# Infini-attention with a gated one-token FFN on one core: sums in a bank each, five jobs per unit, masks two blocks at a time, another clock for the planner, another prologue and output order

## The chip, the cores and the metric

The kernel runs on one core of a Trainium2 chip. The metric is device time in microseconds (us) of one launch; smaller is better. A profile is one execution, with the time of every instruction on each engine: TensorE (PE for matmuls, PEld for its weight loads), VectorE (DVE), ScalarE (ACT), GpSimd (POOL) and SyncE (SP), which here issues all transfers.

## The reference

Two branches over the same 2048 tokens of width 640, mixed by a gate for each token:

```python
x = A_x                                              # [1, 2048, 640]
g = sigmoid((x * gate_w).sum(-1, keepdims=True))
# A: 32 heads of 20 columns, 4 segments of 512 tokens, a memory M, z carried over segments
for s in range(4):
    qs, ks, vs = q[:, :, s], k[:, :, s], v[:, :, s]  # x @ wq, x @ wk, x @ wv
    logits = einsum("bhqd,bhkd->bhqk", qs, ks) * scale + mask
    a_dot = einsum("bhqk,bhkd->bhqd", softmax(logits), vs)
    a_mem = (phi(qs) @ M) / (phi(qs) @ z + 1e-6)
    outs.append(gh * a_mem + (1 - gh) * a_dot)       # gh = sigmoid(beta), by head
    M = M + phi(ks).T @ vs; z = z + phi(ks).sum(tokens)
a = concat(outs) @ wo
# B: the one token with the largest x @ w_r goes through a SwiGLU FFN (640 -> 1728 -> 640)
b = x + scatter(y * sigmoid(r_sel))
out = g * a + (1 - g) * b
```

The mask is additive: -1e9 for `ar[:, None] < ar[None, :]`, that is, for every key that lies behind its query.

## The kernel before

Every matrix is split into a high and a low part (`hi` rounded by ACT, `lo` the difference by DVE or POOL), and a product is the sum of three matmuls: high by high, low by high, high by low.

**Units and jobs.** A unit is half of the heads in one segment: eight units. Its projections (`projections`, `pair_up`) come in four jobs. Jobs 0 and 1 make two tiles each of 128 channels (queries and keys of four heads mixed, `TILES`) by 512 tokens; jobs 2 and 3 each make a half of the fifth channel tile, as two pieces of 128 tokens, and then two blocks of 128 tokens of the values (320 columns, 322 in the first half, where the router and the gate ride along). `pair_up` works on the two halves of the PE array's rows at once: a pair is one matmul on rows 0 to 63 and one on rows 64 to 127, each into a bank of its own; after 15 pairs (5 row blocks by 3 products) the halves change banks, with a drain of PE between them ("swap"), and 15 more pairs follow. Both banks belong to one tile, `sums`.

**Evacuation.** When a job is done, `evac_t` copies the channel tiles to SBUF (ACT for the first bank, L417, DVE for the second, L420), and `evac_v` the values (ACT L518, DVE L522). The next job's first matmul waits for that. High and low parts then go through HBM (`place`, `place_low`, `bring_back`) into `qs` and `ks`, where a group of four heads has its stacked operands; there are five such pairs of buffers.

**Attention.** For each group n (32 in all) five steps `a_step` make the logits in one orientation (L622), add the mask on the diagonal block with four matmuls of 128 columns (L626: `pick` loaded as weights, `tri` streamed), and DVE takes the row maximum (L629). The maxima go through a transpose and four small transfers (`m_rows`, `qs<-mr`) into two more rows of `qs`. Five steps `b_step` then make the transposed logits with the maximum subtracted (L677), ACT exponentiates (L681), POOL masks (L687), and `pv_step` multiplies by the values (L702). Of the five steps of a group, two have one block of 512 columns, two have blocks of 384 and 128, one has two of 256.

**Planner.** The order on every engine is fixed when the program is built: a loop at the end keeps a rough clock for PE, ACT, DVE, POOL and a single transfer stream (`now`), and at each point takes a logit step, a matmul pair of the current job, a pv step, a chore (memory read `nm` and write `mp`, normalisation `otp`, key transposes `ktp`) or a step of the FFN, `Side`. A transfer is issued as soon as its source is due by that clock; SP's own time is not counted. The engines then wait for one another by semaphores.

**Output.** When the FFN has ended, `out_stage` multiplies 16 tiles of 128 tokens by `wo`: rows are fetched back, transposed (`ttp`, L918), split, and multiplied in a `pair_up` of 320 columns a bank; DVE mixes both banks into the output row (L981), one after the other. The transposes of the next tile stand in the swap of the current one.

**Prologue.** The constants (`identf`, `pick`, `tri`, `gate`, `mask4`, memsets) come first on DVE and POOL; the first loads use a ring of four buffers, `raw`.

## Time and profile before

| | us |
|---|---|
| median of 3 runs (787.68 to 788.91) | 787.73 |
| the profiled execution | 790.6 |
| its span, first to last instruction | 788.9 |
| PE busy in the span | 698.2 |
| DVE, ACT, POOL busy | 406.1, 366.0, 267.4 |
| mean granted clock of TensorE | 0.932 |

PE is busy in 88% of the span. A busy time counts from the start of a matmul to the end of its pipeline, so two matmuls overlap; what a matmul costs in a stream is the distance from its start to the next one's start. The granted clock is 1.0 at 2.4 GHz and 0.5 at 1.2 GHz.

### The profile page before, as it was taken

The page shows a single profiled execution, that of the slowest core. Times are in us where ns is not written, and L with a number is a line of the kernel's source. Part 1 is how long each engine was busy: PE and PEld are TensorE (multiplying, and loading weights), DVE is VectorE, ACT ScalarE, POOL GpSimd, SP SyncE. Part 2 cuts the span into 40 slices and gives each one's busy share as a digit, 9 for nine tenths or more (in the row PEclk, how much of TensorE's full clock was granted, in tenths as well). Part 3 has the DMA queues.
Part 4 walks back from the last instruction along what each step waited for, and adds up shares of the span by engine and source line. Part 5 has one row for each costly group of instructions (what it writes and reads, how often), then busy time and mean ns, then how long its engine had stood idle before and what let it go on. Part 6 is the DMA issues. An engine that isn't in the chain of part 4 may idle for free.

```text
span 788.9 us, 19342 instructions
## 1 busy us (share of the span) xinstructions
PE 698.2 (88%) x7860; PEld 576.9 (73%) x7860; DVE 406.1 (51%) x730; ACT 366.0 (46%) x646; POOL 267.4 (34%) x343
## 2 busy tenths in 40 slices
PE   2889999999999999989999898987998959898886
PEld 1678778777877787778778786777777847777675
DVE  7435554554546346464665344662656545553433
ACT  3624545554546356654655354451554425334411
POOL 5514322543244455832533143251445212111100
PEclk9969998999999889999999899995999978999999
DMA  4783545245424554778476536553348644243451
GB/s 118 209 256 111 140 124 145 87 129 145 137 61 105 159 151 129 205 211 223 134 229 208 162 98 199 156 143 108 120 140 229 187 149 124 87 129 123 136 160 51
DMA packets 84912, 116.69 MB, mean 148 GB/s; under 512 B 36624, under 2 KB 48408, under 8 KB 84824
## 3 DMA queue, kind: packets, MB, share of 16 engines
q1 hardware_dynamic: 84824, 115.46, 51.1%
q8 instruction: 62, 1.02, 0.5%
q14 instruction: 26, 0.21, 0.1%
HBM read 72.94 MB, written 41.96 MB: 146 GB/s over the span
## 4 chain that ended last, share of the span: by engine, by line
PE 75%; DMA 9%; DVE 7%; issue 3%; ACT 3%; SPq 1%; POOL 0%; DVEq 0%; ACTq 0%; POOLq 0%
PE sums L359 41%; PE pv L702 8%; PE a L622 5%; PE a L626 5%; PE bt L677 5%; DMA qs<-mr 3%; PE nm L475 3%; PE otp L729 3%; DVE mx L629 2%; PE mp L498 2%; PE ttp L918 1%; DVE xf L981 1%; DMA stkq<-lo 1%; ACT p L681 1%; DMA ks<-stkk 1%
## 5 line engine op out<-in xcount | busy, mean ns | idle before, releaser
L629 DVE TENSOR_REDUCE mx<-a 128x2 f32<-128x1024 f32 (+3 forms) x256 | 202.0, 821 | 177.0 <-PE a L626 175.1
L681 ACT ACTIVATE p<-bt 128x1024 f32<-128x1024 f32 x160 | 164.2, 1027 | 147.2 <-PE bt L677 142.1
L687 POOL TENSOR_SCALAR_AFFINE_SELECT p<-p 128x512 f32<-128x512 f32 (+1 forms) x160 | 88.2, 552 | 294.4 <-ACT p L681 285.7
L359 PE MATMUL sums<-xhi,whi 64*128 64x128 f32 (+1 forms) x640 | 131.8, 371 | 20.9 <-ACT xhi L164 12.2
L359 PE MATMUL sums<-xhi,wlo 64*128 64x128 f32 (+1 forms) x640 | 129.1, 359 | 3.1 <-DVE wlo L167 3.1
L359 PE MATMUL sums<-xlo,whi 64*128 64x128 f32 (+1 forms) x640 | 129.7, 361 | 0.0
L622 PE MATMUL a<-ks,qs 60*128 60x384 f32 (+3 forms) x512 | 100.4, 361 | 22.8 <-DVE mx L629 13.3
L359 PEld LDWEIGHTS sums<-xhi,whi 64*128 64x128 f32 x640 | 79.0, 205 | 34.4 <-issue 13.0
L626 PEld LDWEIGHTS a<-tri,pick 64*128 64x128 f32 x1024 | 100.7, 201 | 3.6
L626 PE MATMUL a<-tri,pick 64*128 64x128 f32 x1024 | 97.4, 264 | 0.0
L677 PE MATMUL bt<-qs,ks 62*128 62x384 f32 (+3 forms) x512 | 81.3, 341 | 15.4 <-DMA qs<-mr 12.8
L622 PEld LDWEIGHTS a<-ks,qs 60*128 60x128 f32 x512 | 59.5, 199 | 37.3 <-issue 21.3
L359 PEld LDWEIGHTS sums<-xhi,wlo 64*128 64x128 f32 x640 | 81.0, 207 | 6.4 <-POOL xlo L167 3.6
L359 PEld LDWEIGHTS sums<-xlo,whi 64*128 64x128 f32 x640 | 81.2, 207 | 5.8 <-POOL xlo L167 0.6
L702 PE MATMUL pv<-p,va 128*32 128x512 f32 (+3 forms) x1024 | 75.5, 435 | 0.4 <-ACT mr L658 0.4
L677 PEld LDWEIGHTS bt<-qs,ks 62*128 62x128 f32 x512 | 53.8, 196 | 24.5 <-DMA qs<-mr 11.7
L429 POOL TENSOR_TENSOR lo<-phi,hi 128x512 fp32r<-128x512 f32 (+1 forms) x48 | 53.1, 1107 | 46.7 <-ACT hi L425 30.4
L359 PE MATMUL sums<-whi,xhi 64*128 64x322 f32 (+1 forms) x320 | 64.1, 366 | 1.6
L359 PE MATMUL sums<-whi,oh 64*128 64x320 f32 x320 | 55.1, 330 | 10.5 <-DVE xf L981 8.3
L702 PEld LDWEIGHTS pv<-p,va 128*32 128x32 f32 x1024 | 30.2, 109 | 43.4 <-issue 35.3
L359 PE MATMUL sums<-wlo,xhi 64*128 64x322 f32 (+1 forms) x320 | 60.8, 342 | 0.0
L359 PE MATMUL sums<-whi,xlo 64*128 64x322 f32 (+1 forms) x320 | 60.7, 340 | 0.0
(110 smaller groups left out, 1096.0 us busy)
## 6 DMA issues: line engine op xcount, KB each, us to landing
qs<-stkq SPq DMA_DIRECT2D x64, 240.0 KB
ks<-stkk SPq DMA_DIRECT2D x64, 240.0 KB
raw<-in_xT_dram SPq DMA_DIRECT2D x40, 256.0 KB
stkq<-hi SPq DMA_DIRECT2D x24, 320.0 KB
otok<-ou SPq DMA_DIRECT2D x32, 160.0 KB
xf<-in_x_dram SPq DMA_DIRECT2D x8, 640.0 KB
out_dram<-xf SPq DMA_DIRECT2D x16, 320.0 KB
wt<-in_wg_dram SPq DMA_DIRECT2D x10, 432.0 KB
```

The costliest lines, as they stand in the source:

```text
L359: nc.tensor.matmul(o, a, b, start=phase == 0 and i == 0, stop=phase == 1 and i == n - 1)
L429: nc.gpsimd.tensor_tensor(out=lo, in0=c, in1=f32(hi), op=OP.subtract)
L475: nc.tensor.matmul(nm[:, c, :], e[:GC, 128 * c:128 * c + 128], mbd[:, g, :], start=True, stop=True)
L498: nc.tensor.matmul(mp[:, g, :], kk[:, g, c, :], va[u % 2][:, c, GW * g:GW * g + GW], start=c == 0, stop=c == 3)
L622: nc.tensor.matmul(a[:, b, at:at + w], q_, ks[n % NS][64 * b:64 * b + ST, p, :w], start=True, stop=False)
L626: nc.tensor.matmul(a[:, b, at + w - 128:at + w], pick[r, h], tri[r, h], start=False, stop=h == 1)
L629: nc.vector.tensor_reduce(out=mx[n][:, :, p, i:i + 1], in_=a[:, :, at:at + w], axis=AX.X, op=OP.max)
L677: nc.tensor.matmul(bt[:, b, at:at + w], k_, qs[n % NS][64 * b:64 * b + ST + 2, p, L - w:], start=True, stop=True)
L681: nc.scalar.activation(pt, bt, AF.Exp, scale=SCALE)
L687: nc.gpsimd.affine_select(out=d, in_=d, pattern=[[0, e[1]] for e in dims[:-1]] + [[1, 128]], base=0, channel_multiplier=-1, compare_op=OP. ...
L702: nc.tensor.matmul(pv[32 * j:32 * j + 32, 128 * c:], va[u % 2][:, c, VW * h:VW * h + 32], pt_tiles[n, j % 2, c][:, j // 2], start=c == 0, ...
L729: nc.tensor.transpose(tp[:, c].rearrange("p j r -> p (j r)"), o[:, 128 * c:128 * c + 128], identf)
```

## The change

- **Two tiles.** `sums` becomes two tiles, `sums` and `sumt`, of one bank each. ACT evacuates the first and DVE the second, for channels and for values alike.
- **Five jobs.** The fifth channel tile has a job of its own, two pieces of 256 tokens; jobs 3 and 4 make the values.
- **Masks.** A step with two blocks adds both masks at once: four matmuls that stream 2 x 128 columns, instead of eight of 128. The step with two blocks of 256 reduces them in one DVE instruction.
- **Clock.** `now` gets SP, and `dma` counts 0.45 us of SP for an issue and bytes by 260 GB/s for the transfer; what follows is due by that. Transfers wait until SP is free by the clock and go by rank, the maxima's first. In the last 1.2 us of a job no logit step is taken. Chores and the FFN's steps have conditions and due times of their own; the FFN no longer has to end before the output stage starts.
- **Prologue.** The first nine loads are issued and split before the constants; the first six use the ring of `p`.
- **Output.** High-part products come first, then the ten with the low part; DVE mixes the first bank while ACT scales the second, and POOL adds that one; transposes for the next tile come before a tile's matmuls or in its swap.

```diff
+PR = 6
+FIRST = 18
+JOBS = 5
...
+    def dma(dst, src, kb):
+
+        nc.sync.dma_start(dst, src)
+        now["SP"] = max(now["SP"], now["PE"]) + 0.45
+        now["DMA"] = max(now["DMA"], now["SP"]) + kb / 260
+        return now["DMA"] + 2.2
...
     def flush_dmas(t):
-        for e in sorted((e for e in dmas if e[0] <= t), key=lambda e: e[0]):
+        while now["SP"] <= t + 0.2:
+            e = min((e for e in dmas if e[1] <= t), key=lambda e: e[:2], default=None)
+            if e is None:
+                break
             dmas.remove(e)
-            e[1]()
+            e[2]()
...
-    sums = psum.tile([128, 2, 512], F32, name="sums")
+    sums = [psum.tile([128, 512], F32, name=n) for n in ("sums", "sumt")]
...
-        dst = c.rearrange("p (a b) -> p a b", a=2) if len(src.shape) == 3 else c
-        if scalar:
-            nc.scalar.copy(dst, src)
-            free = run("ACT", 0.17 + w / 1200, now["PE"])
-        else:
-            nc.vector.tensor_copy(dst, src)
-            free = run("DVE", 0.12 + w / 960, now["PE"])
+        for bank, t0, t1 in parts:
+            if bank == 0:
+                nc.scalar.copy(c[:, t0:t1], sums[0][:, :t1 - t0])
+                end = run("ACT", 0.17 + (t1 - t0) / 1200, now["PE"] + 0.22)
+            else:
+                nc.vector.tensor_copy(c[:, t0:t1], sums[1][:, :t1 - t0])
+                end = run("DVE", 0.15 + (t1 - t0) / 960, now["PE"] + 0.22)
...
+        copy, engine = ((nc.scalar.copy, "ACT"), (nc.vector.tensor_copy, "DVE"))[bank]
+        copy(sub(va[u % 2], c * (HH * VW + 11), [[VW * q, 2], [VW, q], [1, DH]]),
+             sub(acc, 0, [[VC // 2 + (2 if hf == 0 else 0), 2], [DH, q], [1, DH]]))
...
-            for job in range(4):
+            for job in range(JOBS):
...
+                if job < 2:
+                    n, f, g = L, channels(u, 2 * job, 0, L), channels(u, 2 * job + 1, 0, L)
+                elif job == 2:
+                    n, f, g = L // 2, channels(u, 4, 0, L // 2), channels(u, 4, L // 2, L // 2)
+                else:
+                    n, f, g = w, tokens(u, c, w), tokens(u, c + 1, w)
...
+        ends = [at + w - 128 for i, p, at, w in LOGITS[k]]
+        for h in range(2):
+            for b in range(2):
+                r = slice(64 * b, 64 * b + 64)
+                if k < 2:
+                    nc.tensor.matmul(a[:, b, ends[0]:], pick[r, h], tri[r, h], start=False, stop=h == 1)
+                else:
+                    nc.tensor.matmul(sub(a[:, b], min(ends), [[max(ends) - min(ends), 2], [1, 128]]), pick[r, h],
+                                     sub(tri[r, h], 0, [[0, 2], [1, 128]]), start=False, stop=h == 1)
...
-        later_dma(now["ACT"], fn)
+        later_dma(now["ACT"], fn, 0)
...
-                    k, part = divmod(i, 3)
+                    k, part = divmod(i, 2) if i < 2 * KT else (i - 2 * KT, 2)
...
+            nc.vector.scalar_tensor_tensor(out=x0, in0=sums[0][:, :n], scalar=R["gx"][:, t:t + 1], in1=x0,
+                                           op0=OP.mult, op1=OP.add)
...
+            nc.scalar.activation(half, sums[1][:, :n], AF.Copy, scale=R["gx"][:, t:t + 1])
...
+            nc.gpsimd.tensor_tensor(out=x1, in0=half, in1=x1, op=OP.add)
...
     def both():
         yield from projections()
-        for f in side:
-            while f.live:
-                f.step()
         yield from out_stage()
...
+    for _ in range(9):
+        load_next()
+    for _ in range(9):
+        split_next()
+    constants()
+    now["PE"] = at["T", 0, 0]
...
-        if logits(0.0, t):
+        if (where[0] != "mid" or left[0] > 1.2) and logits(0.0, t):
             continue
```

Three places of the order. On PE, the end of unit 1's second job and the start of its third, before (`a` and `bt` are the two logit orientations, `tri` by `pick` the masks):

```order
L359 MATMUL sums<-xlo,whi 128x512 x2
L677 MATMUL bt<-qs_114,ks_115 128x512 x2
L622 MATMUL a<-ks_118,qs_117 128x256 x2
L626 MATMUL a<-tri,pick 128x128 x4
L622 MATMUL a<-ks_118,qs_117 128x256 x2
L626 MATMUL a<-tri,pick 128x128 x4
L677 MATMUL bt<-qs_114,ks_115 128x384 x2
L677 MATMUL bt<-qs_114,ks_115 128x128 x2
L359 MATMUL sums<-xhi,whi 128x128 x2
```

The same place on PE after:

```order
L371 MATMUL sums<-xlo,whi 128x512
L371 MATMUL sumt<-xlo,whi 128x512
L653 MATMUL a<-ks_94,qs_89 128x384 x2
L653 MATMUL a<-ks_94,qs_89 128x128 x2
L662 MATMUL a<-tri,pick 128x2x128 x4
L717 MATMUL bt<-qs_88,ks_93 128x512 x2
L371 MATMUL sums<-xhi,whi 128x256
L371 MATMUL sumt<-xhi,whi 128x256
```

Eight mask matmuls have become four wider ones, the pair behind them has 256 columns instead of 128, and one logit step fewer stands between the two jobs.

On DVE, the last of the constants and the first splits in the prologue, before (`ogate`, `ed`, `mask`, `ks` are constants, `wlo` and `xlo` low parts of the first loads, `phi<-sums` evacuates the first job):

```order
L106 TENSOR_SCALAR ogate<-gate 128x32
L112 TENSOR_SCALAR ed<-jd 80x80
L114 TENSOR_REDUCE mask_106<-ed 80x4
L121 MEMSET ks_109 128x1024
L121 MEMSET ks_115 128x1024
L121 MEMSET ks_121 128x1024
L167 TENSOR_TENSOR wlo<-raw,whi 128x5x48
L167 TENSOR_TENSOR wlo<-raw,whi 128x5x16
L167 TENSOR_TENSOR xlo<-raw,xhi 128x512 x3
```

The start of DVE's queue after:

```order
L175 TENSOR_TENSOR wlo<-raw,whi 128x5x80
L175 TENSOR_TENSOR wlo<-raw,whi 128x5x32
L175 TENSOR_TENSOR wlo<-raw,whi 128x5x80
L175 TENSOR_TENSOR wlo<-raw,whi 128x5x64
L175 TENSOR_TENSOR xlo<-raw,xhi 128x512 x3
L108 TENSOR_SCALAR identf<-jp 128x128
L110 MEMSET ks_92 128x1024
L110 MEMSET ks_94 128x1024
```

The splits have moved ahead of the constants, and the constants now stand ahead of the first job's evacuation on DVE.

On PE, the swap of the last output tile that still has transposes in it, before (`ttp` are the transposes of the next tile's rows):

```order
L359 MATMUL sums<-whi,ol 128x320 x2
L918 MATMUL ttp<-identf,ot 128x128 x4
L918 MATMUL ttp<-identf,ot_10943 128x128
L359 MATMUL sums<-whi,oh 128x320 x2
L359 MATMUL sums<-wlo,oh 128x320 x2
```

The last transposes on PE after:

```order
L371 MATMUL sums<-whi,ol 128x320
L371 MATMUL sumt<-whi,ol 128x320
L964 MATMUL ttp<-identf,ot 128x128 x4
L964 MATMUL ttp<-identf,ot_9891 128x128
L371 MATMUL sums<-whi,oh 128x320
L371 MATMUL sumt<-whi,oh 128x320
```

They have moved from the middle of a tile to the gap between two tiles, and the low parts (`ol`) are the last products of a half.

## Rows read from the trace of the kernel before

**Rows 1.** The page's first part: busy us, share of the span, instructions.

```profile
PE 698.2 (88%) x7860; PEld 576.9 (73%) x7860; DVE 406.1 (51%) x730; ACT 366.0 (46%) x646; POOL 267.4 (34%) x343
```

**Rows 2.** PE's timeline: start us, length us, line, output<-inputs, shape, count, [idle before].

```profile
37.86 0.27 PE L359 MATMUL sums<-xhi,wlo 64*128 64x128 f32 x2
...
39.20 0.28 PE L359 MATMUL sums<-xhi,wlo 64*128 64x128 f32 x2
39.31 0.27 PE L359 MATMUL sums<-xlo,whi 64*128 64x128 f32 x2
39.67 0.33 PE L359 MATMUL sums<-xhi,whi 64*128 64x128 f32 x2
```

**Rows 3.** PE's timeline, a transposed logit step and the projection pair behind it.

```profile
77.05 0.41 PE L677 MATMUL bt<-qs,ks 62*128 62x384 f32 x4
77.29 0.46 PE L359 MATMUL sums<-xlo,whi 64*128 64x512 f32 x2
```

**Rows 4.** PE's timeline, two logit steps with two masks each.

```profile
61.22 0.34 PE L622 MATMUL a<-ks,qs 60*128 60x256 f32 x2
61.40 0.34 PE L626 MATMUL a<-tri,pick 64*128 64x128 f32 x4
...
61.92 0.28 PE L359 MATMUL sums<-xlo,whi 64*128 64x128 f32 x2
...
75.44 0.29 PE L622 MATMUL a<-ks,qs 60*128 60x256 f32 x2
...
76.07 0.46 PE L359 MATMUL sums<-xhi,wlo 64*128 64x512 f32 x2
```

**Rows 5.** PE's timeline around the first job's end.

```profile
26.72 0.41 PE L359 MATMUL sums<-xlo,whi 64*128 64x512 f32 x2
28.53 0.50 PE L359 MATMUL sums<-xhi,whi 64*128 64x512 f32 x2 [1.40 <-DVE phi L420]
```

**Rows 6.** Groups by shape: count | busy us, mean ns of one | idle us before.

```profile
L417 ACT COPY phi<-sums 128x512 f32<-128x512 f32 x16 | 9.3, 584 | 14.9 <-PE sums L359 14.9
L420 DVE COPY phi<-sums 128x512 f32<-128x512 f32 x16 | 11.0, 690 | 16.3 <-ACT phi L417 15.9
```

**Rows 7.** PE's waits: engine, line <- what released it: us, times, longest.

```profile
PE a L622 <- DVE mx L629: 13.3, 9, 7.3
PE bt L677 <- DMA qs<-mr: 12.8, 5, 4.7
PE sums L359 <- DVE xf L981: 8.3, 11, 1.2
PE a L622 <- DVE rg L522: 7.5, 7, 1.5
PE sums L359 <- DVE phi L420: 4.9, 7, 1.4
```

**Rows 8.** Windows at half clock: us, busy (x) PE PEld DVE ACT POOL, PEclk.

```profile
115.62:122.43 6.81, 6.81 (x66) 6.72 (x64) 1.51 (x5) 2.80 (x6) 2.80 (x4) 0.50 0.29 78
...
sum 105.59, PE 92.57 PEld 86.07 DVE 36.44 ACT 32.12 POOL 28.79; mean PE 7.71 PEld 7.17 DVE 3.04 ACT 2.68 POOL 2.40
```

**Rows 9.** The chain that ended last: start us, us, what, count; output tiles.

```profile
769.20 2.48 PE sums L359 x30
...
772.86 2.47 PE sums L359 x30
...
779.79 2.47 PE sums L359 x30
```

**Rows 10.** Timelines of ACT and DVE in the prologue.

```profile
5.11 3.43 ACT L164 CAST whi<-raw 128x400 fp32r<-128x400 f32 x6 [0.75 <-DMA raw<-in_wc_dram]
10.45 0.62 ACT L164 CAST xhi<-raw 128x512 fp32r<-128x512 f32 x1 [1.90 <-DMA raw<-in_xT_dram]
...
1.18 4.48 DVE L89 TENSOR_SCALAR identf<-jp 128x128 f32<-128x128 int32 x1 [1.18 <-POOL jp L87]
...
13.62 0.91 DVE L121 MEMSET ks<- 128x1024 f32 x1 [0.16 <-issue]
```

More of the change, by code (lines that the diff above doesn't have):

```diff
@@ L139, in run @@
+    now = {"PE": 0.0, "ACT": 0.0, "DVE": 0.0, "POOL": 0.0, "SP": 0.0, "DMA": 0.0}
     def run(engine, us, *ready):
@@ L165, in split @@
         end = run("ACT", 0.2 + width / 1200, ready)
-        fast = now["DVE"] + 1.0 < now["POOL"] and key[1] == 0 and key[0] != "O"
+        fast = now["DVE"] + width / 960 < now["POOL"] + width / 430 and issued[0] <= FIRST
         (nc.vector if fast else nc.gpsimd).tensor_tensor(out=lo, in0=raw, in1=f32(hi), op=OP.subtract)
@@ L266, in feed @@
     def feed():
[L268 removed]
+        while room() and max(raw_free[raw_slot()], now["SP"] - 0.2) <= now["PE"]:
             load_next()
@@ L365, in place @@
-    def place(kind, m, c0, hi, r0, n, t0, t1, ready):
+        left[0] = 2 * n * us_of(cols)
+        for phase in range(2):
+            if phase:
+                where[0] = "swap"
+                yield 0.0
+                nc.tensor.drain()
+                pe(0.12)
+            use((64, 128))
+            where[0] = "mid"
+            for i in range(n):
+                for o, f, r in ((o0, f0, phase), (o1, f1, 1 - phase)):
+                    a, b, ready = f(i, r)
+                    pe(0.0, ready)
+                    nc.tensor.matmul(o, a, b, start=phase == 0 and i == 0, stop=phase == 1 and i == n - 1)
+                note(phase, i)
+                left[0] -= us_of(cols)
+                yield pe(us_of(cols)) - 0.22
@@ L902, in out_mix @@
         nc.scalar.activation(xf[t], xf[t], AF.Copy, scale=R["gb"][:, t:t + 1])
-        end = run("ACT", 0.85, now["DMA"])
+        end = run("ACT", 0.85, xf_at[t])
         nc.vector.scalar_tensor_tensor(out=xf[t], in0=R["yb"], scalar=R["oh"][:, t:t + 1], in1=xf[t], op0=OP.mult,
@@ L936, in fetch_rows, with ahead @@
             row_load(t)
-            ot_at[t] = now["PE"] + 3.0
+            return True
+    def ahead(t):
+        fetch_rows(t)
+        fetch_rows(t + 1)
+        if t in ot and ot_at[t] <= now["PE"] and misc_ready(2) <= now["PE"] + 0.4:
+            out_rows(t)
             return True
@@ L1101, in tile_infini_mod @@
         blocked = next_b() is None and done_b[0] < NG
-        old = [e for e in chores if e[0] <= t]
-        if pv and (where[0] == "open" or blocked or gt > 1e8 or left[0] > 2.0):
+        old = [e for e in chores if e[0] <= t and e[-1]()]
+        if pv and (where[0] == "open" or blocked or gt > 1e8 or left[0] > 2.0 or over[0] == JOBS * NU):
             logits(0.2, t)
@@ L1106, in tile_infini_mod @@
             continue
-        if old and where[0] == "swap":
+        waits = t - side_at[0] if side and side[0].last == 2 else -1.0
+        if where[0] == "swap" and (old or waits >= 0.0) and misc_ready() <= t + 0.2:
             logits(0.2, t)
@@ L1116, in tile_infini_mod @@
             continue
-        if logits(0.4 if gt < 1e8 else 99.0, t):
+        if logits(1.0 if gt < 1e8 else 99.0, t):
             continue
-        if old and gt > 1e8:
+        if gt > 1e8 and (old or waits >= 0.0) and misc_ready() <= t:
             visit(9.0, False)
```

408 lines of the change are left out of this document (200 added, 208 removed).

## The prediction

> **What bounds the kernel now.** I read the page's first part, then PE's waits, then PE's timeline. PE is busy for 698.2 of the span's 788.9 us, DVE for 406.1, ACT for 366.0 [rows 1]: PE sets the end, and a microsecond taken from it counts almost in full. Three things make its time long. First, its matmuls: a stream of 128-column pairs moves on by (39.20 - 37.86) / 12 = 0.112 us a pair [rows 2], while the two pairs of a transposed logit step, 512 columns in all, take 77.29 - 77.05 = 0.24 [rows 3], so 0.12 a pair of 256. A 128-column pair costs nearly as much as one of twice the width. Second, waits: 90.7 us in which PE has nothing in it, the largest behind DVE's maxima, the maxima's transfers and the evacuations [rows 7]. Third, the clock: in twelve stretches, together 105.6 us with 92.6 us of PE busy, it is granted at half, 1.2 GHz [rows 8]; at 2.4 GHz that work takes half, so the clock costs 46.3 us.
>
> I sum against the span, 788.9 (device time of that execution 790.6), and take the saving from the median of the runs, 787.73.
>
> **A. The fifth channel tile: -25.** Before: 8 units x 2 jobs x 2 halves x 15 = 480 pairs of 128 columns, 480 x 0.112 = 53.8. After: 240 pairs of 256. No projection pair of 256 is in the trace; the nearest row is the logit pair at 0.12 [rows 3], 28.8 us; the dearest is the pair of 256 ahead of a mask, 61.40 - 61.22 = 0.18 [rows 4], 43.2. So -25.0, between -11 and -25. I take the first: like it, the new pairs follow their own kind. A rule of the Trainium skill weighs against this term: "TensorE: Matmul & The Clock Gate", section "Back-to-back issue gap", gives the isolated spacing as 134 cycles for 128 columns and 262 for 256, with the caution that it leaves out the weight loads; by it two narrow matmuls cost what one wide one does, and A would be under 1 us in an estimate from that page. The trace sides with the caution: 0.112, not half of it.
>
> **B. The masks: -15.** Of 160 steps 96 have two blocks. One costs 0.70 (61.22 to 61.92) or, behind a wide pair, 0.63 (75.44 to 76.07) [rows 4]; mean 0.66. After: the same four logit matmuls, 0.24 as in [rows 3], and two mask pairs of 256 columns at 0.12 to 0.18: 0.48 to 0.60. I take 0.50, since nothing hinders the weights of the second pair: 96 x 0.16 = -15, between -6 and -17. That the moving operand repeats its 128 columns by a stride of zero is not in the trace; if it cost a pair more, the upper end holds.
>
> **C. Drains and changes of shape: +2.** A swap costs 39.67 - 39.31 = 0.36 against 0.11, so 0.25 [rows 2]; one fewer per unit, -2.0. By the order PE changes its tile shape (64 x 128, 128 x 128, 128 x 32) 206 times instead of 165; each at something between nothing and that 0.25, taken at 0.1: +4, at most +10.
>
> **D. Job starts: -6.** Now 1.81 us lie between a job's last pair and the next job's first [rows 5], most of it ACT's copy (584 ns) and then DVE's (690 ns), one after the other [rows 6]. Side by side it is 1.81 - 0.58 = 1.23, of which the pair itself is 0.23. The order puts one or two logit steps there (a step of two masks 0.50, a transposed one 0.24), some 0.7 us, so 0.3 stay open at 40 starts: 12 us, against 4.9 + 7.5 + (13.3 - 7.3) = 18.4 in three rows now [rows 7]. That the last 1.2 us of a job take no logit step keeps an exponential or a maximum from standing ahead of the evacuation. Bounds: -14 if no start waits, +8 if as much again opens.
>
> **E. Output tiles: -11.** A tile of the undisturbed end takes 779.79 - 772.86 = 6.93: two halves of 2.47, a swap, and 772.86 - 771.68 = 1.18 of evacuation [rows 9]. DVE's two equal instructions become one beside ACT, about -0.5, and the transposes fill what is left of that gap instead of widening the swap by some 0.7: -1.1 on each of the last five tiles. On the other eleven, where logit steps fill the gaps, half of that. POOL's addition lies behind the banks' release and hides, but for the last tile's, under 1 us. Bounds -4 and -17 (all sixteen).
>
> **F. Transfers that PE waits for: -13.** 12.8 us are waits of the transposed logits for the maxima's transfers, and 7.3 us one wait of a logit step on DVE [rows 7], whose queue was held by the FFN's last transfer. Both are orders in which the rough clock did not see SP's queue; now it counts SP, sends the maxima first, and issues DVE's addition only when its transfer is due. I take two thirds of 20.1; bounds -5 and -20. What it counts, 0.45 us an issue, may be short.
>
> **G. Prologue: -3.** Now the first activation is cast at 10.45, 1.9 us late, though the weights' casts end at 5.11 + 3.43 = 8.54 [rows 10]; with nine loads under way at once it would follow at 8.54. But the constants, 1.18 to 14.53 on DVE, mostly slowed by POOL's memsets beside them [rows 10], now stand between the splits (done at about 12.5) and the first evacuation. If they take as long as now, the second job starts at about 26.5 instead of 28.53 [rows 5]; if they take half, at about 21. -2 to -8, and nearer to the first, since POOL's memsets run beside them again.
>
> **H. The clock: -24.** Six of the twelve stretches, with over half of their time, begin in or just behind runs of 128-column pairs, and six behind waits of over 1 us. The narrow pairs are gone from the projections, and D and F shorten the waits. I take half of 46.3 for what goes; bounds -8 (only what stems from F) and -40.
>
> **Less cover: +5.** With 40 us less work on PE (A and B) the same chains of other engines are hidden by less. Today 90.7 of 788.9 is open; the same share of 40 is 5.
>
> Sum: -25 - 15 + 2 - 6 - 11 - 13 - 3 - 24 + 5 = -90. From the median: 787.7 - 90 = 698.
>
> **Rivals.** 1. *Only the work goes* (0.20): the planner's new order waits as much as the old one, at other places, and the clock falls as often. Then A, B, C and half of E hold: 787.7 - 43 = 744. For it: 40 job starts instead of 32, less to fill them. Against: the largest waits now have causes in the order that the change addresses. 2. *Job starts pull the clock down* (0.04), slower: at each of the 40 starts PE stands for 0.8 us beyond the present, because the evacuation on either engine finds an exponential or a maximum ahead of it, and every second start brings a half-clock stretch of 6.81 [rows 8], at 3.4 us. D and H are then not gained (787.7 - 60 = 728), and 32 + 68 come on top: 828. It ends slower than before from 60 us on, at 0.6 us a start and 11 such stretches. For it: short waits precede half of today's stretches. Against: the evacuation is shorter. The Trainium skill states the mechanism, in "TensorE: Matmul & The Clock Gate", section "A second HAM failure mode: psum-queue depth-cycling": short idles of PE between groups that cycle through PSUM banks make the clock oscillate; the present trace has stretches that begin so. 3. *The wide pairs cost twice the narrow ones* (0.03): A and B give nothing, 698 + 40 = 738. 4. *Nearly all waits and stretches go* (0.06): C to H at their good ends, 656.
>
> **How the numbers follow.** The forecast, 664 to 725, has 0.67; the five shares add to 1. The range for 8 in 10 takes in rival 3 and the lower half of rival 1: 664 to 740. What a measurement of this kernel can tell from no change is about 0.2%. Faster 0.95; same 0.01; slower 0.04, rival 2.
>
> **What would show it.** A: pairs of 256 columns at 0.12 from start to start. B: a step of two masks at 0.50. D: ACT's and DVE's copies side by side, and sums of PE's waits for them at 12 us or less. E: tiles at the end of 5.8 us. F: no wait of a transposed logit step for `qs<-mr` over 2 us, none of 7 on DVE. G: the first matmul at about 9.2, the second job at 26. H: half-clock stretches of 40 to 60 us in all. PE's busy time should fall to about 630. I am wrong if PE's idle time stays at 90 (rival 1), if it grows with the number of jobs (rival 2), or if half-clock time does not shrink.

## The result, and the profile after

The changed kernel takes 671.15 us (median of 4 runs, 670.5 to 676.57) against 788.32 us for the kernel before in the same runs: a ratio of 0.8516, 95% interval 0.8458 to 0.8574. The forecast was 698, with 664 to 740 as range; the time lies inside, 27 us below the forecast. Device time of the profiled execution is 670.66 us, its span 668.3.

The first part of the page after, which answers to [rows 1] (busy us, share of the span, instructions):

```profile
PE 618.0 (92%) x6996; PEld 497.9 (75%) x6996; DVE 401.5 (60%) x675; ACT 366.6 (55%) x638; POOL 278.3 (42%) x350
```

PE still sets the end. Its idle time is 668.3 - 618.0 = 50.3 us instead of 90.7. The stretches at half clock, as windows (us; busy (x instructions) of PE, PEld, DVE, ACT, POOL; granted clock; share of DMA; GB/s), answer to [rows 8]:

```profile
22.51:29.34 6.83, 3.78 (x20) 3.12 (x22) 4.22 (x9) 2.68 (x6) 1.28 (x1) 0.50 0.65 190
83.95:87.36 3.41, 3.41 (x22) 2.18 (x24) 2.31 (x5) 2.43 (x3) 0.75 (x2) 0.50 0.94 266
234.13:240.96 6.83, 4.93 (x36) 4.85 (x38) 3.16 (x4) 5.49 (x9) 4.07 (x5) 0.50 0.54 136
268.27:271.68 3.41, 3.31 (x19) 2.83 (x21) 2.26 (x9) 0.00 (x0) 2.04 (x3) 0.50 0.24 49
sum 20.48, PE 15.43 PEld 12.97 DVE 11.94 ACT 10.60 POOL 8.15; mean PE 3.86 PEld 3.24 DVE 2.99 ACT 2.65 POOL 2.04
```

Four stretches are left of twelve, 20.5 us instead of 105.6, with 15.4 us of PE busy instead of 92.6 (one that begins 0.7 us before the end, when PE is done, is left out here and below). At 2.4 GHz that work takes half, so the clock now costs 7.7 us instead of 46.3. The first matmuls of either kernel go at half pace as well (in the changed one 0.43 us a pair of 512 columns at 11.2 us, 0.23 from 12.4 us on), but the profile has 1.0 there, so they count as full clock in what follows. The span divides in three:

| us | before | after | difference |
|---|---|---|---|
| PE idle | 90.7 | 50.3 | -40.4 |
| cost of the half clock (half of PE's busy time in it) | 46.3 | 7.7 | -38.6 |
| PE busy, the rest (its work at full clock) | 651.9 | 610.3 | -41.6 |
| span | 788.9 | 668.3 | -120.6 |

A third each: work, waits, clock. The work was forecast (A, B, C: -38); of waits and clock less was expected (D to H with less cover: -52, against -79).

PE's waits after (engine, line <- what released it: us in total, times, longest), which answer to [rows 7]:

```profile
PE sums L371 <- ACT xhi L172: 8.8, 1, 8.8
PE bt L717 <- ACT p L721: 8.1, 5, 5.2
PE sumt L371 <- DVE phi L428: 6.2, 1, 6.2
PE mtp L697 <- DVE mneg L685: 5.3, 7, 1.0
PE ktp L492 <- DVE phi L455: 3.0, 3, 1.4
PE sums L371 <- ACT phi L425: 2.0, 3, 0.7
PE a L653 <- DVE mx L666: 0.3, 1, 0.3
```

The five rows of [rows 7] are all but gone: no wait of `bt` for `qs<-mr`, 0.3 instead of 13.3 for the maxima, no wait for `rg` that counts, 2.0 for the evacuation outside one wait of 6.2, and for the output's evacuation 1.7 instead of 8.3 (1.4 for ACT's `half`, 0.3 for DVE's addition). In their place stand the exponential (8.1, before 2.4), the transposes of the maxima (5.3) and those of the keys (3.0).

### The profile page after: what moved, and what is told of

The parts are those of the page before. It is cut to its first block, busy times and chain, and to the rows that moved or that the text cites. A ratio compares the mean times of both kernels' runs of the same rounds, so it can differ in the third digit from the quotient of the medians.

```text
span 668.3 us, 17482 instructions
## 1 busy us (share of the span) xinstructions
PE 618.0 (92%) x6996; PEld 497.9 (75%) x6996; DVE 401.5 (60%) x675; ACT 366.6 (55%) x638; POOL 278.3 (42%) x350
## 3 DMA queue, kind: packets, MB, share of 16 engines
q1 hardware_dynamic: 81240, 115.46, 59.5%
## 4 chain that ended last, share of the span: by engine, by line
PE 73%; DVE 10%; DMA 6%; issue 4%; SPq 2%; ACT 2%; POOL 2%; POOLq 0%; ACTq 0%; DVEq 0%
PE sums L371 23%; PE sumt L371 14%; PE pv L742 10%; PE a L653 5%; PE bt L717 5%; PE a L662 4%; PE nm L503 3%; SPq L147 2%; PE otp L769 2%; DVE mx L666 2%; DMA stkk<-lo 2%; PE mp L527 2%; DMA stkk<-hi 2%; PE a L660 1%; DVE mneg L685 1%
## 5 line engine op out<-in xcount | busy, mean ns | idle before, releaser
L670 DVE TENSOR_REDUCE mx<-a 128x2 f32<-128x768 f32 (+1 forms) x192 | 160.6, 865 | 68.0 <-PE a L662 43.9
L371 PE MATMUL sums<-xhi,whi 64*128 64x512 f32 (+1 forms) x240 | 91.5, 381 | 12.9 <-ACT xhi L172 8.8
L371 PE MATMUL sumt<-xhi,whi 64*128 64x512 f32 (+1 forms) x240 | 92.0, 384 | 6.2 <-DVE phi L428 6.2
L371 PE MATMUL sums<-xhi,wlo 64*128 64x512 f32 (+1 forms) x240 | 88.8, 370 | 0.0
L371 PE MATMUL sums<-xlo,whi 64*128 64x512 f32 (+1 forms) x240 | 88.3, 368 | 0.1
L371 PE MATMUL sumt<-xhi,wlo 64*128 64x512 f32 (+1 forms) x240 | 88.2, 368 | 0.0
L371 PE MATMUL sumt<-xlo,whi 64*128 64x512 f32 (+1 forms) x240 | 88.2, 368 | 0.0
L438 POOL TENSOR_TENSOR lo<-phi,hi 128x512 fp32r<-128x512 f32 x40 | 52.3, 1308 | 46.1 <-ACT hi L434 27.5
L717 PEld LDWEIGHTS bt<-qs,ks 62*128 62x128 f32 x512 | 50.3, 188 | 16.7 <-ACT p L721 9.7
L666 DVE TENSOR_REDUCE mx<-a 128x4 f32<-128x1024 f32 x32 | 39.2, 1224 | 27.7 <-PE a L662 27.7
L371 PE MATMUL sums<-whi,oh 64*128 64x320 f32 x160 | 50.3, 323 | 4.0 <-ACT half L1036 1.4
L371 PE MATMUL sumt<-whi,xhi 64*128 64x322 f32 (+1 forms) x160 | 53.5, 334 | 0.0
```

Of the source, the lines that this page charges most:

```text
L371: nc.tensor.matmul(o, a, b, start=phase == 0 and i == 0, stop=phase == 1 and i == n - 1)
L438: nc.gpsimd.tensor_tensor(out=lo, in0=c, in1=f32(hi), op=OP.subtract)
L666: nc.vector.tensor_reduce(out=mx[n][:, :, :, 1], in_=a.rearrange("p b (c t) -> p b c t", c=2), axis=AX.X, op=OP.max)
L670: nc.vector.tensor_reduce(out=mx[n][:, :, p, i:i + 1], in_=a[:, :, at:at + w], axis=AX.X, op=OP.max)
L717: nc.tensor.matmul(bt[:, b, at:at + w], k_, qs[n % NS][64 * b:64 * b + ST + 2, p, L - w:], start=True, stop=True)
```

## The experiments

All times below are medians of 4 to 6 runs; spans and the rest come from one profiled execution each, which can lie up to 5 us from its median. The kernel before, measured again each time, had medians between 787.6 and 795.1 us, so a difference of less than about 1% between two kernels is not to be read from their times alone (the prediction had put this at 0.2%). "Work" is PE's busy time less half of what of it lies at half clock.

| kernel | us | span | PE idle | half clock (PE busy in it) | work |
|---|---|---|---|---|---|
| changed | 671.15 | 668.3 | 50.3 | 20.5 (15.4) | 610.3 |
| masks one block at a time | 688.44 | 685.1 | 49.6 | 20.5 (14.9) | 628.1 |
| narrow pairs in job 2 | 687.36 | 686.8 | 44.7 | 23.9 (17.4) | 633.4 |
| both of these | 706.45 | 708.1 | 46.2 | 23.9 (19.5) | 652.2 |
| sums in one tile | 687.91 | 687.2 | 66.7 | 23.9 (19.0) | 611.0 |
| old clock for transfers | 685.44 | 685.5 | 59.5 | 44.4 (34.9) | 608.6 |
| no rule for a job's end | 688.16 | 687.4 | 60.6 | 37.6 (30.0) | 611.8 |
| constants first | 674.62 | 676.7 | 55.6 | 23.9 (19.8) | 611.2 |
| constants late | 668.45 | 667.0 | 49.8 | 17.1 (11.1) | 611.7 |
| long waits added | 692.02 | 692.5 | 61.8 | 40.9 (37.7) | 611.9 |
| constants cut in two | 669.82 | 667.9 | 45.6 | 27.3 (25.2) | 609.7 |
| more low parts on DVE | 688.81 | 681.9 | 59.1 | 30.7 (23.1) | 611.3 |
| constants cut, some low parts on DVE | 668.91 | 669.6 | 47.5 | 23.9 (21.7) | 611.3 |

### The work of PE: masks and narrow pairs

Masks apart:

```diff
         for i, p, at, w in LOGITS[k]:
...
-        for h in range(2):
-            for b in range(2):
-                r = slice(64 * b, 64 * b + 64)
-                if k < 2:
...
+            for h in range(2):
+                for b in range(2):
+                    r = slice(64 * b, 64 * b + 64)
+                    nc.tensor.matmul(a[:, b, at + w - 128:at + w], pick[r, h], tri[r, h], start=False, stop=h == 1)
```

> The changed kernel with the masks of a two-block step added one block at a time again (eight matmuls of 128 columns instead of four of 2 x 128); the order on all engines is otherwise that of the changed kernel. Theory (term B is work of PE and nothing else): a two-block step goes from about 0.52 to about 0.66 us, 96 x 0.14 = +13, so 671 + 13 = 684, half-clock time within 7 us of the changed kernel's 21. Rival 1 (the narrow mask pairs also pull the clock down): more than 40 us at half clock and 695 or more. Rival 2 (the masks lie beside other waits, B gives nothing): 671 to 675.

Narrow pairs, in `pair_up`:

```diff
-                for o, f, r in ((o0, f0, phase), (o1, f1, 1 - phase)):
-                    a, b, ready = f(i, r)
-                    pe(0.0, ready)
-                    nc.tensor.matmul(o, a, b, start=phase == 0 and i == 0, stop=phase == 1 and i == n - 1)
+                w = 128 if cols == 256 else cols
+                for c0 in range(0, cols, w):
+                    for o, f, r in ((o0, f0, phase), (o1, f1, 1 - phase)):
...
+                        if w < cols:
+                            o, b = o[:, c0:c0 + w], b[:, c0:c0 + w]
```

> The changed kernel with each projection matmul of 256 columns (job 2) cut into two of 128, in the same order otherwise: 480 pairs of 128 columns instead of 240 of 256, as before the change. Theory (term A is work, and the runs of narrow pairs were what six of the twelve half-clock stretches began in): 240 x (2 x 0.112 - 0.12) = +25 of work, and six stretches of some 5 us come back, +13: about 709, half-clock time about 50 us. Rival (narrow pairs are work only, the clock follows the waits): 671 + 25 = 696, half-clock time about 21 us.

Both edits at once:

> Both of the two edits before: masks one block at a time and narrow pairs in job 2. Theory (two separate pieces of work): the sum of the two single losses within 4 us; 722 if the clock falls with the narrow pairs as expected there, 709 by work alone. Rival (they act on the clock together): more than 8 us beyond the sum, with half-clock time above the sum of the two.

Measured: +17.3 us for the masks (the theory's side), +16.2 for the narrow pairs (the rival's side in the clock, and less than either had put), +35.3 for both (the sum, by work alone). PE's timeline (start us, length us, line, output<-inputs, shape, count), first a two-block step of the changed kernel, then one with the masks apart, each with what follows it:

```profile
111.14 0.41 PE L653 MATMUL a<-ks,qs 60*128 60x384 f32 x4
111.38 0.45 PE L662 MATMUL a<-tri,pick 64*128 64x256 f32 x4
111.67 0.31 PE L371 MATMUL sums<-wlo,xhi 64*128 64x322 f32 x1
```

```profile
161.30 0.45 PE L653 MATMUL a<-ks,qs 60*128 60x384 f32 x2
161.49 0.44 PE L657 MATMUL a<-tri,pick 64*128 64x128 f32 x4
161.66 0.38 PE L653 MATMUL a<-ks,qs 60*128 60x128 f32 x2
161.77 0.48 PE L657 MATMUL a<-tri,pick 64*128 64x128 f32 x4
161.99 0.33 PE L371 MATMUL sums<-xhi,whi 64*128 64x256 f32 x1
```

The step shown takes 111.67 - 111.14 = 0.53 us against 161.99 - 161.30 = 0.69. Times 96 that is 15.4; the work column says 628.1 - 610.3 = 17.8. The pairs of job 2, in the changed kernel and then cut:

```profile
229.36 0.28 PE L371 MATMUL sumt<-xhi,whi 64*128 64x256 f32 x1
...
230.31 0.28 PE L371 MATMUL sumt<-xlo,whi 64*128 64x256 f32 x1
```

```profile
161.39 0.27 PE L375 MATMUL sums<-xhi,wlo 64*128 64x128 f32 x1
...
163.06 0.27 PE L375 MATMUL sums<-xlo,whi 64*128 64x128 f32 x1
```

Eight pairs of 256 columns in 0.95 us, 0.119 each; fifteen of 128 in 1.67, 0.111 each. The work column gives 633.4 - 610.3 = 23.1, of which 5.6 came back as less idle time.

What matters most in these three runs is what did not happen. With all narrow pairs back, and with the masks too, the half-clock time is 23.9 us, not the 50 expected; its stretches stand where they stood. So narrow pairs by themselves do not pull the clock down, as term H had it. Five of the eight runs of narrow pairs have no wait of 0.4 us or more beside them, so this does not say what narrow pairs do together with waits. The work is additive (35.3 against 17.3 + 16.2).

### What pulls the clock down

Seven waits were added where neither narrow pairs nor masks stand:

```diff
-                nc.vector.tensor_copy(c[:, t0:t1], sums[1][:, :t1 - t0])
+                for _ in range(4 if u and j == 1 else 1):
+                    nc.vector.tensor_copy(c[:, t0:t1], sums[1][:, :t1 - t0])
```

> The changed kernel with DVE's copy of the second bank made four times instead of once at the end of the first job of units 1 to 7: seven waits of PE of some 2 us more, no narrow pair, and the order otherwise unchanged. Theory (the clock falls behind waits of PE, of whatever width the pairs are): idle time from 50 to about 64 us, and a half-clock stretch of 3.4 us or more behind most of the seven, together 45 us or more: 671 + 14 + 10 to 20, 695 to 705. Rival (waits cost their own length and the clock falls for another reason): idle time about 64 us, half-clock time within 7 us of 21, 685.

Measured: 692.0, idle time +11.5, half-clock time doubled. Its waits for the copy, and two of its half-clock windows with the sum of all:

```profile
PE sumt L371 <- DVE phi L429: 15.2, 6, 6.1
```

```profile
149.16:152.57 3.41, 3.41 (x26) 3.04 (x24) 1.29 (x2) 1.54 (x2) 0.64 (x1) 0.50 0.48 144
...
442.70:446.11 3.41, 3.41 (x22) 1.96 (x22) 2.00 (x5) 0.13 (x1) 0.00 (x0) 0.50 0.09 14
sum 40.94, PE 37.68 PEld 27.92 DVE 18.72 ACT 15.79 POOL 10.06; mean PE 4.19 PEld 3.10 DVE 2.08 ACT 1.75 POOL 1.12
```

Apart from the wait of 6.1 that the changed kernel has too, there are five new ones, (15.2 - 6.1) / 5 = 1.8 us each (two of the seven copies stayed covered). Four of the five have a stretch of 3.41 us behind them, among matmuls of 512 columns, at 74, 149, 296 and 443 us; behind the fifth none came. Most of the rest of the new half-clock time belongs to waits of 1.5 and 1.7 us for key transposes, at 46 and 332 us. Not each wait of this length has a stretch: one of 1.58 us for `col` at 267 us has one in the changed kernel, and the same wait, at 279 us in this run, has none. The waits cost 11.5 us themselves and (37.7 - 15.4) / 2 = 11.1 through the clock: as much again. The theory holds; five waits opened instead of seven, and the time fell short of the 695 to 705 expected.

The contrast is the next run, in which the evacuation was put back into one tile, with the planner unchanged:

```diff
-    sums = [psum.tile([128, 512], F32, name=n) for n in ("sums", "sumt")]
+    both_banks = psum.tile([128, 2, 512], F32, name="sums")
+    sums = [both_banks[:, 0], both_banks[:, 1]]
```

> The changed kernel with both banks of the sums in one tile again; the planner's clock and costs are the changed kernel's, which count the two copies as made side by side. Theory (D and E come from copies on two engines at once): ACT's and DVE's copies go one after the other, 0.6 us later at 40 job starts and 16 output tiles, less what the logit steps between still cover: +15 to +30, 686 to 701, PE's idle time from 50 to 65 or more, and the half-clock time, which followed no narrow pairs in the three runs before, grows with it to 50 us or more. Rival (what the planner puts between two jobs covers the longer evacuation too): under +5, idle time within 3 us.

Its waits, and the group of DVE's copies (count | busy us, mean ns | idle us before):

```profile
PE sums L372 <- DVE phi L429: 17.4, 18, 6.1
PE sums L372 <- ACT half L1037: 6.1, 8, 1.3
```

```profile
L429 DVE COPY phi<-sums 128x512 f32<-128x512 f32 x16 | 11.1, 691 | 26.0 <-ACT phi L426 26.0
```

DVE waits for ACT's copy again, and PE's idle time grows by 16.4 us, spread over many waits of mostly 0.7 us (a few of 1.2 to 1.4 among them). It costs 16.8 us, little more than its own length: half-clock time goes from 20.5 to 23.9, which is (19.0 - 15.4) / 2 = 1.8 us of clock. So the first half of the theory held (687.9, inside 686 to 701) and the second, that any more idle time brings the clock down, fell. 16.4 us in short pieces nearly left the clock alone; 11.5 us with five pieces of 1.8 doubled the time at half clock. The Trainium skill, in "TensorE: Matmul & The Clock Gate", section "A second HAM failure mode: psum-queue depth-cycling", tells of a kernel whose clock oscillates through short idles between groups that cycle through PSUM banks; with idles of 0.7 us beside wide pairs no run here shows that. The kernel before has three stretches that begin behind idles of 0.5 to 0.7 us, all beside narrow pairs (see term H below).

### The planner's clock and rule

```diff
-        now["SP"] = max(now["SP"], now["PE"]) + 0.45
-        now["DMA"] = max(now["DMA"], now["SP"]) + kb / 260
+        now["DMA"] = max(now["DMA"], now["PE"]) + kb / 260
...
-        dmas.append((rank, ready, fn))
+        dmas.append((0, ready, fn))
```

> The changed kernel with a planner that counts no time of SP and sends transfers in the order in which they come due, without rank. Theory (F): PE waits again for the maxima's transfers, 10 to 15 us, and the half clock follows these waits: 671 + 13 to 30, 684 to 701. Rival (SP keeps up in either order, since five jobs and the other due times moved the transfers): within 4 us of 671.

Measured: 685.4, as expected in size, but not in its cause. No wait of PE for `qs<-mr` came back at all. The added waits are those for maxima:

```profile
PE a L652 <- DVE mx L665: 5.0, 3, 4.3
PE a L652 <- DVE mx L669: 3.7, 5, 1.3
```

With the wait of 4.3, at 528 us, a half-clock stretch of 10.2 begins. In sum idle time costs 9.2 us more and the clock (34.9 - 15.4) / 2 = 9.8 (the profiled execution is 2.8 us slower than the median).

```diff
-        if (where[0] != "mid" or left[0] > 1.2) and logits(0.0, t):
+        if logits(0.0, t):
```

> The changed kernel without the rule that no logit step is taken in the last 1.2 us of a job. Theory (the rule keeps maxima and exponentials from standing ahead of the evacuation): 40 starts lose some 0.3 us each, 12 us, and waits for the copies, 2 us now, come to 10 or more: 680 to 690. Rival (the copies have engines of their own and the rule does nothing): within 3 us of 671.

Measured: 688.2, inside the theory's 680 to 690, but only in part through the copies. Three rows carry it:

```profile
PE bt L717 <- ACT p L721: 12.3, 13, 5.1
PE sumt L371 <- DVE phi L428: 9.0, 2, 5.2
PE a L653 <- DVE mx L670: 5.5, 10, 1.0
```

The waits for the copies rose by 3, those of logit steps for one another (the exponential, the maximum) by 9. That the steps come closer together without the rule, and wait for the engines that they share, is a reading of these rows and not tested. Idle time +10.3, clock (30.0 - 15.4) / 2 = +7.3.

One more planner edit moved the order: low parts of loads go to DVE where the planner sees POOL behind.

```diff
-        fast = now["DVE"] + width / 960 < now["POOL"] + width / 430 and issued[0] <= FIRST
+        fast = now["DVE"] + width / 960 < now["POOL"] + width / 430 and (issued[0] <= FIRST or now["POOL"] > ready + 1.0)
```

> The changed kernel with low parts of loads given to DVE also in the body, where the planner sees POOL over 1 us behind; the order moves everywhere with it. Theory (the wait of 5.2 us at 231 us and the half-clock stretch behind it come from a POOL queue that is 6 us long): that wait and that stretch go, 671 - 7 = 664. Rival (DVE, which is fuller than POOL, takes the delay over, in maxima and copies): 671 or more, with waits on DVE's maxima of over 5 us in all.

Measured: 688.8, the rival's side: waits for exponentials 10.8 us, for maxima 5.5. The wait at 231 us is gone, and others stand at 517 us (4.1) and at 390, 531 and 536 (2.1 each). Three edits of the planner with three different aims all cost 14 to 18 us. Each moves hundreds of rows of PE's order, so a loss in one of them shows that this order is worse, and only its waits show why; how much of e.g. the 14.3 belongs to SP's time, and how much to any other order, stays open. The runs that leave PE's order alone (masks, pairs, one tile, constants, long waits) do not have this doubt.

### The prologue

Constants ahead of the splits, loads still first:

```diff
-    for _ in range(9):
-        split_next()
-    constants()
+    constants()
+    for _ in range(9):
+        split_next()
+    run("POOL", 4.5)
+    run("DVE", 5.5)
```

> The changed kernel with the constants ahead of the first splits again on DVE, ACT and POOL, the nine loads still first on SP; the order of PE is the same. Theory (the new prologue trades a later first matmul for a wait of 6 us at the second job): the first matmul comes at 13 to 16 us instead of 8.8, the second job at about 24 to 27 as now, so 671 to 675, with about as much idle time before 30 us as in the changed kernel. Rival (the order of the prologue is worth its whole 5 us): 676 or more.

Measured: 674.6. The time alone, 0.5% from 671.15, does not decide between the two; PE's starts do, and they are on the theory's side. PE's starts there, and a row of DVE ahead of the splits:

```profile
15.07 0.79 PE L369 MATMUL sums<-xhi,whi 64*128 64x512 f32 x1 [15.07 <-ACT xhi L170]
...
26.70 0.50 PE L369 MATMUL sums<-xhi,whi 64*128 64x512 f32 x1 [0.67 <-ACT phi L423]
```

```profile
11.27 0.18 DVE L122 TENSOR_SCALAR gate<-gate 128x32 f32<-128x32 f32 x1 [4.43 <-ACT gate L121]
```

The first matmul comes at 15.07 us instead of 8.77, the second job at 26.70 instead of 25.56: what the changed prologue gains at the first job it loses at the second, all but 1.1 us. The constants themselves took less time here, but DVE then stood for 4.43 us ahead of the splits, since the load of `gate` is behind nine others on SP. The rest of the longer span (this profile is 4.9 us above its median) came later: the second unit starts at 61.6 us instead of 55.8, behind a wait of 4.3 us for a key transpose at 47 us, where the changed kernel waits 1.1.

Constants behind the first evacuation, then cut in two:

```diff
                     evac_t(u, 2 * job + 1, [(1, 0, L)])
+                    if u == job == 0:
+                        later_constants(jp)
```

> The changed kernel with DVE's constants queued behind its copy of the first job's second bank instead of ahead of it; the order of PE is the same. Theory (the 6.2 us in which PE waits for that copy are all due to the constants, and the half-clock stretch at 22.5 us comes from that wait): the second job starts at about 19.3 instead of 25.6, the stretch goes, 671 - 8 = 663. Rival (the constants only move the wait to what stands behind them: the key transposes, the first logit steps): a gain under 2 us, with new waits of 4 us or more before 60 us.

```diff
     def later_constants(jp):
         nc.vector.tensor_scalar(identf, jp, 0.0, None, op0=OP.is_equal)
-        for t in ks[::2]:
-            nc.vector.memset(f32(t), 1.0)
+        nc.vector.memset(f32(ks[0]), 1.0)
+        pieces.append(lambda: last_constants(jp))
```

> The changed kernel with DVE's constants cut in two: the identity and the first memset right behind the copy of the first job's second bank, the rest behind what the first key transposes need; the order of PE is the same. Theory (the wait of 6 us is the constants' own length on DVE and hides once it stands ahead of nothing that PE waits for soon): no wait over 1.5 us between the first matmul and 46 us, the half-clock stretch before 30 us gone: 671 - 8 = 663. Rival (PE's start is held by transfers and splits as well, so that it waits elsewhere): 667 or more.

and with some low parts moved from POOL to DVE, the order of PE unchanged:

```diff
-        (nc.vector if fast else nc.gpsimd).tensor_tensor(out=lo, in0=raw, in1=f32(hi), op=OP.subtract)
+        on_dve = fast or key[0] == "T" and (key[1] == 1 or 9 < issued[0] <= FIRST)
+        (nc.vector if on_dve else nc.gpsimd).tensor_tensor(out=lo, in0=raw, in1=f32(hi), op=OP.subtract)
```

> The kernel with the constants cut in two, and on top of it the low parts of some channel weights (loads 10 to 18, and those of the second half of the heads) made by DVE instead of POOL; the order of PE, of ACT, and of the rest is the same. Theory (both waits of over 2 us that this kernel still has behind the first matmul, 2.5 us for a key transpose at 21 us and 5.2 us for an exponential at 230 us, come from low parts queued on POOL, and each pulls the clock down): both waits under 1.5 us, PE's idle time about 41 instead of 45.6 us, half-clock time under 15 instead of 27 us: 660 to 663. Rival (DVE's added work delays maxima and copies by as much, or the clock falls at shorter waits as well): 667 to 671, with half-clock time above 20 us.

Measured: 668.45, 669.82, 668.91: the second and third as their rivals had it, the first close to its own (a gain of 2.7 us where under 2 was put). In the changed kernel PE waits 6.2 us for DVE's copy, queued behind the constants. With the constants late that wait is gone, and this row stands instead:

```profile
PE ktp L494 <- DVE phi L457: 7.7, 3, 6.2
```

the same 6.2 us, now for the instruction of DVE that stands behind the constants for the key transposes. Cut in two, the wait shrinks to 2.5 us and idle time by 4.7, but the half-clock stretch stays and now falls on work:

```profile
22.74:32.98 10.24, 9.50 (x46) 7.29 (x48) 7.60 (x18) 3.42 (x9) 2.52 (x4) 0.50 0.75 229
```

PE is busy for 9.5 us of it, in the changed kernel for 3.8 of 6.83. The clock costs (25.2 - 15.4) / 2 = 4.9 us more: what the wait gave, the clock took. A stretch that lies in a wait is free; the same stretch on matmuls costs half of its length. With the low parts moved as well, the stretch before 30 us is gone, and the second half of the constants delays the next copy instead (on ACT the activation for `gate` stands ahead of it and waits 5.0 us for its transfer); a stretch follows at 34 us:

```profile
PE sums L378 <- ACT phi L432: 3.5, 3, 2.2
```

The wait at 230 us shrinks only from 5.2 to 3.2 us. None of the three is told apart from the others by its runs; they lie 0.2 to 0.4% below the changed kernel's 671.15, less than its own runs scatter (670.5 to 676.57). A version that clearly beats it was not found.

## Why the prediction was right, and where its steps were not

| term | forecast | measured | from |
|---|---|---|---|
| A, wide pairs | -25 | -23.1 of work, 16.2 us of time | narrow pairs |
| B, masks | -15 | -17.8 of work, 17.3 us of time | masks apart |
| C, drains and shapes | +2 | about -1 with all else (-41.6 + 40.9) | work column |
| D, job starts | -6 | -16 | waits |
| E, output | -11 | -9.9, not E alone | stage: 137.5 to 127.6 |
| F, transfers | -13 | -20 | waits |
| G, prologue | -3 | -3.0 | second job at 25.56 instead of 28.53 |
| H, clock | -24 | -38.6 | windows |
| less cover | +5 | about +14, not cover alone | waits |

The rows come from different views and overlap, so they are no second sum.

**A, B, C** were right in kind and size (B came out just past its bound of -17). The nearest row (0.12 for the logit pair) gave the pair of 256 almost exactly (0.119), and the pair of 128, 0.111, costs nearly as much. By the rule that was weighed there, of the Trainium skill ("TensorE: Matmul & The Clock Gate", section "Back-to-back issue gap"), two narrow matmuls would cost what one wide one does; the trace does not agree, and its caution on weight loads stands. B's step measures 0.53 where 0.50 was put, its old form 0.69 where 0.66 was.

**D** was mis-sized. I left 0.3 us open at each of 40 starts, 12 us in all; and my best case, -14 if no start waits, did not fit my own three rows, which add to 18.4. In fact 2.0 us are left (ACT's `phi`) besides the one wait of 6.2 at the constants, which is a matter of the prologue. The 18.4 us of the three old rows became about 2.5. The timelines of ACT and DVE at the end of a job in the third unit show the two copies side by side, and 8 to 12 matmuls of logit steps between two jobs cover them at most starts:

```profile
137.95 0.59 ACT L425 COPY phi<-sums 128x512 f32<-128x512 f32 x1 [1.09 <-PE sums L371]
...
137.98 0.69 DVE L428 COPY phi<-sumt 128x512 f32<-128x512 f32 x1 [0.53 <-PE sums L371]
```

Putting both banks into one tile took back 16.8 us, starts and output together.

**E** held for the last tiles: the last three follow each other at 5.74 us instead of 6.93, where 5.8 was forecast; the two distances before them are 6.29 and 6.47. The stage as a whole is no clean measure, since it holds 1415 matmuls after and 1352 before. PE's timeline, the transposes for the next tile in two successive tiles:

```profile
646.39 0.77 PE L964 MATMUL ttp<-identf,ot 128*128 128x128 f32 x5
...
652.13 0.77 PE L964 MATMUL ttp<-identf,ot 128*128 128x128 f32 x5
```

**F** had its result and not its mechanism. Both waits are gone, -20 instead of -13, but with the old clock for transfers put back, none of the 12.8 us for `qs<-mr` returned. What took them away lies in the rest of the new order, and is not shown.

**G** came out as the sum said, for the reason that it gave: the constants again took long beside POOL. DVE's timeline in the prologue after:

```profile
12.84 4.17 DVE L108 TENSOR_SCALAR identf<-jp 128x128 f32<-128x128 int32 x1
...
24.83 0.68 DVE L428 COPY phi<-sumt 128x512 f32<-128x512 f32 x1
```

The first job's last matmul starts at 17.8 us, the copy of its second bank comes at 24.83: that is the wait of 6.2.

**H** is the step that failed most, -24 against -38.6. It gave half of the stretches to narrow pairs and half to waits, and took half of the cost as a guess between. Narrow pairs put back without waits cost 1.0 us of clock, (17.4 - 15.4) / 2; so the half that H gave to them has no support as it stood. In the trace of before, waits do stand ahead of the six stretches that I gave to the narrow pairs: three behind waits of 1.2, 2.0 and 2.3 us, and three, at 115.6, 194.1 and 269.2 us, behind waits of 0.5 to 0.7. PE's timeline ahead of these three [rows 8]:

```profile
108.39 0.50 PE L677 MATMUL bt<-qs,ks 62*128 62x384 f32 x4 [0.54 <-ACT p L681]
109.60 0.33 PE L359 MATMUL sums<-xhi,whi 64*128 64x128 f32 x2 [0.70 <-DVE phi L420]
...
113.92 1.12 PE L475 MATMUL nm<-mbd,phi 80*128 80x84 f32 x8 [0.53 <-ACT num L478]
...
188.41 0.33 PE L359 MATMUL sums<-xhi,whi 64*128 64x128 f32 x2 [0.68 <-DVE phi L420]
...
192.28 1.12 PE L475 MATMUL nm<-mbd,phi 80*128 80x84 f32 x8 [0.53 <-ACT num L478]
...
268.12 0.33 PE L359 MATMUL sums<-xhi,whi 64*128 64x128 f32 x2 [0.65 <-DVE phi L420]
```

Narrow jobs came in pairs with a start each, so narrow runs and waits for the evacuation stood side by side; which of the two a stretch belongs to could not be read from their place alone. All twelve stretches of before, by the waits in them or just ahead of them (us):

| stretches at | waits | PE busy at half clock | cost, half of it |
|---|---|---|---|
| 351, 447, 488, 532, 641 | 2.0 to 7.3 | 43.3 | 21.7 |
| 41, 71, 232, 314 | 1.2 to 1.5 | 22.6 | 11.3 |
| 116, 194, 269 | 0.5 to 0.7 | 26.6 | 13.3 |

The first line's waits are F's, but for one of the FFN. If its stretches went with them, as the long waits that were added suggest, that alone is 21.7 us, nearly what H took for the whole. For the other two lines the cause is not shown. Short waits put back beside wide pairs cost 1.8 us of clock, narrow pairs put back without waits 1.0, and no run puts both back. The trace of before narrows it: runs of narrow pairs with no wait of 0.4 us or more (at 368, 423, 603 and 623 us) or with a single one of 0.5 to 0.9 (at 133, 212, 293 and 511 us) have no stretch; the three of the last line have two or three such waits within 8 us ahead of them. Whether these close waits would do it without narrow pairs is open.

**Less cover** was too small: the exponential (8.1), the transposes of the maxima (5.3) and of the keys (3.0) now wait for 16.4 us in all, where the same rows of before had 2.4. But 5.2 of them are the one wait at 231 us, for a copy held up by POOL (last section); how much of the rest is cover is not shown.

Of the rivals, the first (only the work goes, 744) is refuted by the idle time of 50.3 us. The second (job starts pull the clock down) has its mechanism shown in the run with long waits, on a kernel whose starts had been made long; at the length that it named, 0.8 us, the run with one tile speaks against it. The third (wide pairs cost twice the narrow ones) falls with 0.119 us. The fourth, 656 with nearly all waits and stretches gone, had 0.06 and was nearer to the measured time than the forecast: 15 us above it instead of 27 below. D, F and H came out at their good ends together. At least F and half of H are one thing, and I had added them as if each could fail alone. That the time still lies in the range owes something to its width: the lower end is only 7 us away.

## What to carry to other kernels

Before a low clock is put down to the instructions that run in it, look at what PE did just ahead: here each wait of more than 2.1 us behind the first job lay in a half-clock stretch or just ahead of one, waits between 1 and 2.1 us in some cases, a spread of 0.7-us waits beside wide matmuls hardly, and narrow matmuls without waits not at all. Short waits close together, among narrow matmuls, stood ahead of three stretches; what they do without them is not shown. So a long wait is to be priced at its length plus half of PE's busy time in the stretch that comes with it, and terms for waits and clock belong together in a sum and in a range. And where a planner sets the order, test a part of it by an edit that leaves the order alone; an edit of the planner's costs shows first of all that another order is another kernel.

## What the runs showed of the hardware that was not expected

An instruction of DVE can take many times its usual time beside a busy POOL. In the body of the changed kernel, one of 38 equal instructions, of which 31 take 0.68 or 0.69 us and six 0.8 to 1.6, lasted 6.47, while POOL worked without a gap (timelines of DVE and of POOL):

```profile
228.72 6.47 DVE L455 SCALAR_TENSOR_TENSOR phi<-phi,neg 128x512 f32<-128x512 f32 x1
```

```profile
228.66 0.91 POOL L539 TENSOR_TENSOR mbd<-mbd,mt 80x336 f32<-80x336 f32 x1
229.53 2.67 POOL L175 TENSOR_TENSOR wlo<-raw,whi 128x80 fp32r<-128x80 f32 x4
232.17 1.25 POOL L175 TENSOR_TENSOR xlo<-raw,xhi 128x512 fp32r<-128x512 f32 x1
233.39 1.25 POOL L438 TENSOR_TENSOR lo<-phi,hi 128x512 fp32r<-128x512 f32 x1
```

It ended at 235.19 us, 0.55 after the last of POOL's instructions shown and beside the next one, a mask. In the prologue `identf` took 4.17 us beside POOL's memsets and 0.30 with the constants late; with the constants first it took 0.94, also beside POOL's memsets, so the loss is not the same each time. The Trainium skill says, in "GPSIMD Engine Reference", section "1. Specifications", that POOL's way into SBUF is shared with DVE, with contention for DVE instructions that read two inputs from SBUF or run in a two-port mode; the instruction of 6.47 us has two such inputs, and the trace agrees; `identf` reads one input, and no run shows whether the same holds for it. ACT's next copy of a bank waited 4.4 us for the last of these rows, PE 5.2 us for the exponential behind that copy, and the half-clock stretch at 234 us begins in that wait.
